# Batch 1's attention scores in one piece, and its softmax one slot sooner, in a fused attention and feed-forward kernel

## The chip, the cores and the metric

One core of a Trainium2 chip runs the whole kernel. The metric is the device time of one execution in microseconds; the figure shown is the median of several runs.

## The reference

Everything is fp32. There are 8 batches of 8 heads, 576 tokens and 64 columns a head, and 32 memory slots for each head. The input arrays are `q`, `k`, `v`, `phi`, `w_in` and `w_out`.

```
a      = softmax(phi) over the 576 tokens
k_m    = a^T k,   v_m = a^T v                       (32 x 64 a head)
attn   = softmax(q k_m^T / 8) over the 32 slots
x      = attn v_m, heads side by side               (4608 x 512)
out    = silu(x w_in) w_out                         (w_in 512 x 2048, w_out 2048 x 512)
```

## The kernel before, in words

**Folding.** `attn v_m` is never formed. `v_m w_in` (256 memory rows by 2048 columns) is made for each batch by `p_mm`, so that the first layer is `ffn1`: the transposed attention (two groups of 128 rows by 576 tokens) against that product. To keep fp32's accuracy with fast matmuls, operands are split into a high and a low part, and three matmuls (high high, high low, low high) stand for one. The splits are work for ScalarE (high) and VectorE (low).

**Slots.** A batch is 16 slots, one for each 128 of the 2048 hidden columns `fc`. A slot has 12 matmuls `ffn1(fc)` (L634) into the PSUM tile `h`, the SiLU of `h` on ScalarE (L657 into `g`, L659 into `gleft`, for the 64 tokens beyond 512), the split of `g` on VectorE (cast L649, subtract L651, into `gparts`), and 12 matmuls of the second layer (L673), for the slot before, into four accumulators. `h` is one tile of two PSUM banks: the next `ffn1` must wait for `gleft` (L659) to have read it, and for whoever else reads the space beside it.

**What stands between.** At times given in slots and half slots, a table `events` puts in the attention of the next batch: phi's softmax, `e_mm` (k_m and v_m, L327 and L335), `e_tr` (their transpose `kvT`, written beside `h`, read from there by VectorE, L358, and by ScalarE, L359), the scores, the softmax over memory slots (`s_max` L416, `s_sub` L420, `s_exp` L424 on ScalarE, `s_sum` L428 to 430, `s_norm` L434), the transposes back (`s_back` L447) and the split of the result. `p_mm` makes the next columns of the folded product in the PSUM tile `bg`, which exists once and which `p_mm`, `e_mm` of batch 1 and the scores share. Batch 0 has its own times (`at_slot`, L718), since in it the weights are also still being loaded and converted: they come as 64-bit words, and `w_conv` (L166 to 177) turns each piece into fp32 by two ScalarE steps (L167, L169), two or three VectorE steps (L171, L173, L177), and for `w_out` the high half `wo_hi` (L175) on ScalarE. The weight pieces go through three buffers, and a new load is issued as one is free.

**Scores.** For batches 2 to 7, `s_all` makes them in one go in slot 10: 288 + 224 columns in `bg`, the last 64 beside `h`, then four transposes on VectorE. For batch 1, `s_mm` makes them in two halves of 288 columns, each through `bg`, in slots 9.5 and 11.5, each followed by two transposes (L402). A half of `q` is loaded by `load_q`; the second half of batch 1's comes in slot 7.5.

**Order.** TensorE's order is that of the program (`in_order(PE)`). So is SyncE's, which issues nearly all DMAs, and, from batch 1 on, ScalarE's. In batch 0 a scheduler orders what VectorE and ScalarE do. In batch 0 events of a whole slot come after two of the four tiles of the second layer (`finish`), those of a half slot after all four.

Of the kernel before, what the change touches and what calls it, by code (L numbers as in the profile page):

```python
# [10 lines left out]
F32 = mybir.dt.float32  # L11
# [8 lines left out]
P = 128  # L20
B, S, H, M, D = 8, 576, 8, 32, 64
HM = H * M
NR = H // 2
# [6 lines left out]
HALF = S // 2  # L30
# [18 lines left out]
def attn_ffn_kernel(  # L49
# [9 lines left out]
    nc = tc.nc  # L59
    const = ctx.enter_context(tc.tile_pool(name="const", bufs=1))  # L60
    sb = ctx.enter_context(tc.tile_pool(name="sb", bufs=2))
# [24 lines left out]
    def load(dst, src, few=False, queue=None):  # L86
        i = (queue or nc.sync).dma_start(dst, src)
        if few:
            tc.add_manual_dep(
                i.ins,  # L90
                loads[-DEEP].ins.name,
                mybir.DependencyInfo(mybir.DependencyClass.Sync, mybir.DependencyReason.DATA),
                reason="few at a time",
            )
        loads.append(i)
# [18 lines left out]
    def bgtile():  # L114
        return ps.tile([P, 2, 512], F32, tag="bg", name="bg", bufs=1)
# [88 lines left out]
    at = [dict() for _ in range(B)]  # L204
    live = {}

    def banks(b):
        if b == 0:
            return [ps.tile([P, 512], F32, tag="acc", name=f"first{i}", bufs=NI) for i in range(2)]
        bg = bgtile()  # L210
        return [bg[:, 0], bg[:, 1]]

    def beside_h(w):

        return [live["h"][:, i, HALF : HALF + w] for i in range(2)]
# [10 lines left out]
    def load_kv(b):  # L226
        queue = nc.scalar if b == 0 else None
        ts = []
        for c in range(FULLC):
            t = sb.tile([P, 2, NR, KVW], F32, tag="kv", name=f"kv{b}_{c}", bufs=FULLC)  # L230
            load(t.rearrange("p g r f -> p (g r f)"), kv[b, :, c * KVC : (c + 1) * KVC], queue=queue)
            ts.append(t)
        t = sb.tile([P, NR, KVW], F32, tag="kr", name=f"kr{b}", bufs=1)
        load(t.rearrange("p r f -> p (r f)"), kv[b, :, FULLC * KVC :], queue=queue)
        at[b]["kv"], at[b]["kr"] = ts, t

    def load_q(b, hf, few=False):
        t = sb.tile([P, NR, HALF], F32, tag="q", name=f"q{b}_{hf}", bufs=2)
        at[b]["q", hf] = t
        load(t.rearrange("p r s -> p (r s)"), qT[b, hf], few)  # L240
# [121 lines left out]
    def s_all(b):  # L362

        sc = at[b]["sc"] = sb.tile([P, 2, S], F32, tag="att", name=f"sc{b}")
        bg, left = bgtile(), beside_h(S - 512)
        kvT = at[b]["kvT"]
        w = 512 - HALF
        for hf, f, n in ((0, 0, HALF), (1, 0, w), (1, w, HALF - w)):
            for r in range(NR):
                for p in range(2):  # L370
                    to = left[p] if f else bg[:, p, hf * HALF : hf * HALF + n]
                    nc.tensor.matmul(  # L372
                        to[M * r : M * (r + 1)],
                        kvT[D * p : D * (p + 1), 0, r],
                        at[b]["q", hf][D * p : D * (p + 1), r, f : f + n],
                        start=True, stop=True, skip_group_check=True,
                    )
        for p in range(2):
            nc.vector.transpose(sc[:, p, :512], bg[:, p])
        for p in range(2):  # L380
            nc.vector.transpose(sc[:, p, 512:], left[p])

    def s_mm(b, hf):
        if "sc" not in at[b]:
            at[b]["sc"] = sb.tile([P, 2, S], F32, tag="att", name=f"sc{b}")
        pt = banks(b)
        kvT, q = at[b]["kvT"], at[b]["q", hf]
        for r in range(NR):
            for p in range(2):
                nc.tensor.matmul(  # L390
                    pt[p][M * r : M * (r + 1), :HALF],
                    kvT[D * p : D * (p + 1), 0, r],
                    q[D * p : D * (p + 1), r],
                    start=True, stop=True, skip_group_check=True,
                )
        at[b]["sp", hf] = pt
        if b:
            s_turn(b, hf)

    def s_turn(b, hf):  # L400
        for p in range(2):
            nc.vector.transpose(at[b]["sc"][:, p, hf * HALF : (hf + 1) * HALF], at[b]["sp", hf][p][:, :HALF])  # L402

    def s_view(b, u):
        return at[b]["sc"][:, :, u[0] : u[1]].rearrange("p g (n m) -> p g n m", m=M)
# [183 lines left out]
    def p_mm(b, f, w, low=True):  # L589
        j = f // JW  # L590
        if f % JW == 0:
            pj[b, j] = [pparts[:, k, j % 2].rearrange("p (g f) -> p g f", g=2) for k in range(2)]
        hi, lo = pj[b, j]
        c = slice(f % JW, f % JW + w)
        bg = bgtile()
        kvT = at[b]["kvT"]
        for r in range(NR):
            for p in range(2):
                nc.tensor.matmul(  # L599
                    bg[M * r : M * (r + 1), p, :w].rearrange("p (k f) -> p k f", f=P),  # L600
                    kvT[D * p : D * (p + 1), 1, r],
                    win[D * p : D * (p + 1), f // P : (f + w) // P, r],
                    start=True, stop=True, skip_group_check=True,
                )
        if low:
            p_split(b, f, w, bg)
        return bg
# [97 lines left out]
    def ev(b, slot, fn, *a):  # L705
        events.setdefault((b, slot), []).append((fn, a))

    for b in range(B):
        n = b + 1
        if b == 0:  # L710
            for j in range(2, DFF // CW):
                ev(b, 2 * j - 1.5, p_mm, b, j * CW, CW)
        else:
            for j in range(1, NJ):
                ev(b, 4 * j - 3, p_mm, b, j * JW, JW)
        if n == B:
            continue
        at_slot = (4, 5, 6, 7.5, 9, 9.5, 11.5, 11.5, 12, 12.5, 12.5, 13) if b == 0 else (1, 2, 3, 5, 9, 10, 10, 11, 12, 13, 13, 14)  # L718
        mx, sub, ex, em, tr, s0, s1, sx, se, ss, sn, sk = at_slot
        ev(b, mx, phi_max, n)  # L720
        if n == 1:
            ev(b, sub, phi_allmax, n, (0, 1), (0,))
            ev(b, sub + 0.5, phi_allmax, n, (0, 1), (1,))
        else:
            for i in range(3):
                ev(b, sub, phi_fold, n, i)
        ev(b, sub + 0.5, phi_sub, n)
        ev(b, ex, phi_exp, n)
        ev(b, em, e_mm, n)
        if n + 1 < B:  # L730
            ev(b, 14 if b == 0 else em + 1, load_kv, n + 1)
        ev(b, tr, e_tr, n)
        ev(b, em, load_q, n, 1)
        if n == 1:
            ev(b, s0, s_mm, n, 0)
            ev(b, s1, s_mm, n, 1)
        else:
            ev(b, s0, s_all, n)
        if n + 1 < B:
            ev(b, s1, load_q, n + 1, 0)  # L740
        ev(b, sx, s_max, n, ALL)
        ev(b, sx, s_sub, n, ALL)
        ev(b, se, s_exp, n, ALL)
        ev(b, ss, s_sum, n, ALL)
        ev(b, sn, s_norm, n, ALL)
        ev(b, sk, s_back, n, ALL)
        ev(b, sk, s_low, n, ALL)
        if n + 1 < B:
            ev(b, sk, load_phi, n + 1)
        ev(b, 14, p_mm, n, 0, JW)  # L750
# [13 lines left out]
    with in_order(DVE, ACT) as last:  # L764
# [56 lines left out]
        bg = p_mm(0, 0, CW, False)  # L821
# [34 lines left out]
    load_next()  # L856
    load_kv(1)
    load_q(1, 0)
    for e in (DVE, ACT):
        whole.enter_context(tc.issue_after(last[e]))  # L860

# [36 lines left out]
def build(arrays, bacc, num_devices=1):  # L898
    nc = bacc.Bacc("TRN2", target_bir_lowering=False, num_devices=1, dynamic_dma_scratch_size=1024)
    aps = [  # L900
        nc.dram_tensor(n, a.shape, mybir.dt.from_np(a.dtype), kind="ExternalInput").ap() for n, a in arrays.items()
    ]
    out = nc.dram_tensor("out", (B * S, DMODEL), F32, kind="ExternalOutput").ap()
    with tile.TileContext(nc) as tc:
        attn_ffn_kernel(tc, *aps, out)
    return nc
# [44 lines left out]
```

## Time and profile before

| | before |
|---|---|
| median of 3 runs | 704.92 us (704.52 to 708.04) |
| the profiled execution | 704.6 us |
| its span, first to last instruction | 702.8 us |
| TensorE (PE) busy | 690.1 us, 98% |
| VectorE (DVE) busy | 366.1 us, 52% |
| ScalarE (ACT) busy | 258.7 us, 37% |
| HBM traffic | 49.95 MB read, 9.44 MB written |

A busy share is that of the whole span. Batch 0 takes the first 110 us or so, and VectorE and ScalarE are far busier in it than later: VectorE 4.96 of the 5 us from 95 to 100, for instance. A PE that is busy is issuing matmuls, which are pipelined; a row of the timeline merges neighbours (x12), its second number is the time until the last of them ends, and the time from one row's start to the next is what a stage costs. PEld is the weight load of a matmul.

### The profile page before, as it was taken

How to read it: one execution, taken by the hardware profiler on the slowest of the kernel's cores; microseconds unless marked ns; L12 is line 12 of the kernel's file. 1: busy time of each engine (PE TensorE's matmuls, PEld its weight loads, DVE VectorE, ACT ScalarE, POOL GpSimd, SP SyncE). 2: the span in 40 equal slices, each digit the busy share in tenths (PEclk: the TensorE clock that was granted, in tenths of full speed). 3: DMA queues.
4: the chain of work that ended last, by engine and by line, in shares of the span. 5: the costliest groups of instructions: out<-in, count | busy, mean ns of one | idle time of the engine just before them, and what ended most of it. 6: DMA issues, size and time to landing. Idle time of an engine off the chain costs nothing.

```text
span 702.8 us, 11778 instructions
## 1 busy us (share of the span) xinstructions
PE 690.1 (98%) x4924; PEld 562.7 (80%) x4924; DVE 366.1 (52%) x667; ACT 258.7 (37%) x455; POOL 0.7 (0%) x6
## 2 busy tenths in 40 slices
PE   8899989999999999999999999999999999999997
PEld 3578768888888888888888888888888888888885
DVE  4898796525745256634636346552564525623322
ACT  3779574413414124431413224341341412431211
POOL 0000000000000000000000000000000000000000
PEclk9999999999999999999999999999999999999999
DMA  9895726122210321131110311112121000010002
GB/s 334 306 341 188 254 78 230 36 102 68 71 39 12 126 68 35 61 137 54 48 61 16 136 39 55 71 40 97 68 76 34 1 1 1 1 61 1 1 0 76
DMA packets 25445, 60.15 MB, mean 86 GB/s; under 512 B 2096, under 2 KB 10416, under 8 KB 25392
## 3 DMA queue, kind: packets, MB, share of 16 engines
q1 hardware_dynamic: 24448, 56.63, 22.7%
q10 hardware_dynamic: 944, 2.77, 1.1%
q8 instruction: 39, 0.64, 0.4%
q14 instruction: 14, 0.11, 0.0%
HBM read 49.95 MB, written 9.44 MB: 85 GB/s over the span
## 4 chain that ended last, share of the span: by engine, by line
PE 85%; DVE 1%; ACT 0%; issue 0%; ACTq 0%
PE acc L673 46%; PE h L634 26%; PE accleft L673 6%; PE bg L599 4%; PE h L327 2%; PE bg L372 1%; PE h L335 0%; PE h L357 0%; ACT L657 0%; DVE sc L420 0%; DVE wo_lo L177 0%; DVE raw L173 0%; PE h L372 0%; ACT wo_hi L175 0%; DVE sc L402 0%
## 5 line engine op out<-in xcount | busy, mean ns | idle before, releaser
L673 PE MATMUL acc<-wo_hi,gparts 128*128 128x512 f32 x1024 | 342.1, 395 | 0.9 <-DVE gparts L651 0.5
L673 PEld LDWEIGHTS acc<-wo_hi,gparts 128*128 128x128 f32 x1024 | 192.2, 188 | 53.9 <-issue 6.6
L634 PEld LDWEIGHTS h<-aparts,pparts 128*128 128x128 f32 x1524 | 214.0, 188 | 15.0 <-issue 2.5
L634 PE MATMUL h<-aparts,pparts 128*128 128x288 f32 x1524 | 223.1, 295 | 1.5 <-ACT gleft L659 1.2
L657 ACT ACTIVATE g<-h 128x512 f32<-128x512 f32 x127 | 76.0, 598 | 348.7 <-PE h L634 179.8
L673 PE MATMUL acc<-wo_lo,gparts 128*128 128x512 f32 x512 | 201.0, 393 | 0.6 <-DVE wo_lo L177 0.6
L649 DVE CAST gparts<-g 128x512 fp32r<-128x512 f32 x128 | 54.5, 426 | 261.3 <-ACT g L657 261.2
L673 PEld LDWEIGHTS acc<-wo_lo,gparts 128*128 128x128 f32 x512 | 96.1, 188 | 18.3 <-DVE wo_lo L177 1.9
L651 DVE TENSOR_TENSOR gparts<-g,gparts 128x512 fp32r<-128x512 f32 x128 | 88.2, 689 | 10.6 <-DVE gparts L649 0.5
L615 DVE TENSOR_TENSOR pparts<-bg,pparts 128x1024 fp32r<-128x1024 f32 (+1 forms) x36 | 39.7, 1102 | 5.2 <-ACT pparts L613 4.8
L673 PE MATMUL accleft<-wo_hi,gparts 128*128 128x512 f32 x128 | 40.6, 390 | 0.0
L613 ACT ACTIVATE pparts<-bg 128x1024 fp32r<-128x1024 f32 (+1 forms) x36 | 33.6, 932 | 14.2 <-PE bg L599 14.1
L599 PE MATMUL bg<-win,kvT 64*32 64x512 f32 (+1 forms) x576 | 35.8, 554 | 0.0
L673 PEld LDWEIGHTS accleft<-wo_hi,gparts 128*128 128x128 f32 x128 | 24.0, 188 | 4.9
L659 ACT ACTIVATE gleft<-h 128x64 f32<-128x64 f32 x127 | 27.8, 219 | 0.0
L681 ACT ACTIVATE o<-acc 128x512 f32<-128x512 f32 x32 | 19.2, 599 | 21.9 <-PE acc L673 10.6
L673 PE MATMUL accleft<-wo_lo,gparts 128*128 128x512 f32 x64 | 24.9, 390 | 0.0
L657 ACT ACT_TABLE_LOAD x14 | 18.0, 1283 | 14.3 <-issue 13.8
L649 DVE CAST gparts<-gleft 128x512 fp32r<-128x512 f32 x16 | 6.8, 427 | 20.7 <-PE accleft L673 12.2
L169 ACT ACTIVATE raw<-raw 128x1024 int32<-128x1024 uint32 (+1 forms) x16 | 16.7, 1041 | 0.0
L327 PEld LDWEIGHTS h<-kv,phi 128*32 128x32 f32 x384 | 10.2, 110 | 5.0 <-ACT gleft L659 5.0
L673 PEld LDWEIGHTS accleft<-wo_lo,gparts 128*128 128x128 f32 x64 | 12.0, 188 | 2.4
(143 smaller groups left out, 366.1 us busy)
## 6 DMA issues: line engine op xcount, KB each, us to landing
kv<-in_kv SPq DMA_DIRECT2D x28, 516.0 KB, 5.6
q<-in_q SPq DMA_DIRECT2D x16, 576.0 KB, 4.9
out<-o SPq DMA_DIRECT2D x32, 256.0 KB, 2.1
raw<-in_w_in SPq DMA_DIRECT2D x14, 512.0 KB, 6.3
raw<-in_w_out SPq DMA_DIRECT2D x6, 1024.0 KB, 5.5
phi<-in_phi SPq DMA_DIRECT2D x7, 576.0 KB, 3.5
kv<-in_kv ACTq DMA_DIRECT2D x4, 516.0 KB, 6.7
kr<-in_kv SPq DMA_DIRECT2D x7, 258.0 KB, 6.6
```

The costliest lines, as they stand in the source:

```text
L169: i = nc.scalar.activation(r, low, AF.Copy, scale=2.0**-29)
L327: nc.tensor.matmul(pt[p][M * r : M * (r + 1), :KVW], e[:, p, c, M * r : M * (r + 1)], kvt[c][:, p, r], start=c == 0, stop=False, skip_grou ...
L599: nc.tensor.matmul(bg[M * r : M * (r + 1), p, :w].rearrange("p (k f) -> p k f", f=P), kvT[D * p : D * (p + 1), 1, r], win[D * p : D * (p + ...
L613: nc.scalar.activation(hi[:, :, c], bg[:, :, :w], AF.Copy)
L615: nc.vector.tensor_tensor(lo[:, :, c], bg[:, :, :w], hi[:, :, c], op=ALU.subtract)
L634: nc.tensor.matmul(h[:, hf, :HALF], wt[:, p, fs], a[:, p, hf * HALF : (hf + 1) * HALF], start=n[hf] == 0, stop=n[hf] == 5, skip_group_chec ...
L649: nc.vector.tensor_copy(ghi, g32)
L651: nc.vector.tensor_tensor(glo, g32, ghi, op=ALU.subtract)
L657: nc.scalar.activation(g32.rearrange("p (h f) -> p h f", h=2), h[:, :, :w], AF.Silu)
L659: i = nc.scalar.activation(gleft[:, fc, o : o + LEFT].rearrange("p (h f) -> p h f", h=2), h[:, :, w:HALF], AF.Silu)
L673: nc.tensor.matmul(acc[key], gt[:, cs], wt[:, fc], start=fc == 0 and n == 0, stop=fc == NFC - 1 and n == 2)
L681: nc.scalar.activation(o[:, :w], a[:, :w], AF.Copy)
```

## The change

Batch 1's scores are made by `s_all` too, in slot 10, so `s_mm` and `s_turn` go. `s_all` traces the transposes of the 64 columns beside `h` ahead of those of `bg` for batch 1. The softmax's steps of batch 1 move in the table for batch 0: `s_max` and `s_sub` from 11.5 to 10.5, the exp from 12 to 11, sum and normalise from 12.5 to 12; the way back stays at 13. The second half of batch 1's `q` is loaded right behind the first, ahead of the loop.

```diff
--- before.py
+++ after.py
@@ -375,31 +375,10 @@
                         at[b]["q", hf][D * p : D * (p + 1), r, f : f + n],
                         start=True, stop=True, skip_group_check=True,
                     )
-        for p in range(2):
-            nc.vector.transpose(sc[:, p, :512], bg[:, p])
-        for p in range(2):
-            nc.vector.transpose(sc[:, p, 512:], left[p])
-
-    def s_mm(b, hf):
-        if "sc" not in at[b]:
-            at[b]["sc"] = sb.tile([P, 2, S], F32, tag="att", name=f"sc{b}")
-        pt = banks(b)
-        kvT, q = at[b]["kvT"], at[b]["q", hf]
-        for r in range(NR):
+        parts = [(slice(512, S), left), (slice(0, 512), [bg[:, p] for p in range(2)])]
+        for cols, src in parts if b == 1 else parts[::-1]:
             for p in range(2):
-                nc.tensor.matmul(
-                    pt[p][M * r : M * (r + 1), :HALF],
-                    kvT[D * p : D * (p + 1), 0, r],
-                    q[D * p : D * (p + 1), r],
-                    start=True, stop=True, skip_group_check=True,
-                )
-        at[b]["sp", hf] = pt
-        if b:
-            s_turn(b, hf)
-
-    def s_turn(b, hf):
-        for p in range(2):
-            nc.vector.transpose(at[b]["sc"][:, p, hf * HALF : (hf + 1) * HALF], at[b]["sp", hf][p][:, :HALF])
+                nc.vector.transpose(sc[:, p, cols], src[p])
 
     def s_view(b, u):
         return at[b]["sc"][:, :, u[0] : u[1]].rearrange("p g (n m) -> p g n m", m=M)
@@ -715,7 +694,7 @@
                 ev(b, 4 * j - 3, p_mm, b, j * JW, JW)
         if n == B:
             continue
-        at_slot = (4, 5, 6, 7.5, 9, 9.5, 11.5, 11.5, 12, 12.5, 12.5, 13) if b == 0 else (1, 2, 3, 5, 9, 10, 10, 11, 12, 13, 13, 14)
+        at_slot = (4, 5, 6, 7.5, 9, 10, 10, 10.5, 11, 12, 12, 13) if b == 0 else (1, 2, 3, 5, 9, 10, 10, 11, 12, 13, 13, 14)
         mx, sub, ex, em, tr, s0, s1, sx, se, ss, sn, sk = at_slot
         ev(b, mx, phi_max, n)
         if n == 1:
@@ -730,12 +709,9 @@
         if n + 1 < B:
             ev(b, 14 if b == 0 else em + 1, load_kv, n + 1)
         ev(b, tr, e_tr, n)
-        ev(b, em, load_q, n, 1)
-        if n == 1:
-            ev(b, s0, s_mm, n, 0)
-            ev(b, s1, s_mm, n, 1)
-        else:
-            ev(b, s0, s_all, n)
+        if b:
+            ev(b, em, load_q, n, 1)
+        ev(b, s0, s_all, n)
         if n + 1 < B:
             ev(b, s1, load_q, n + 1, 0)
         ev(b, sx, s_max, n, ALL)
@@ -856,6 +832,7 @@
     load_next()
     load_kv(1)
     load_q(1, 0)
+    load_q(1, 1)
     for e in (DVE, ACT):
         whole.enter_context(tc.issue_after(last[e]))
 
```

The table `at_slot` and the scheduler set what these lines do to the queues; so here is the order on the two engines concerned, before and after (line numbers are each file's own; in the changed file the lines from `s_view` on are 21 less).

ScalarE, from the SiLU of slot 11 to `gleft` of slot 12. `g` and `gleft` are the SiLU's two results; `win`, `raw`, `cva` and `wo_hi` belong to the weights' conversion; `sc` is the exp of the softmax; numbers behind a name count buffers. Before:

```order
L657 ACTIVATE g_933<-h 128x512
L659 ACTIVATE gleft<-h 128x64
L167 ACTIVATE win<-raw 128x1024
L169 ACTIVATE raw<-raw 128x1024
L167 ACTIVATE cva<-raw 128x1024
L169 ACTIVATE raw<-raw 128x1024
L175 ACTIVATE wo_hi<-cva 128x1024
L657 ACTIVATE g_990<-h 128x512
L659 ACTIVATE gleft<-h 128x64
```

ScalarE, the same place after the change:

```order
L636 ACTIVATE g_956<-h 128x512
L638 ACTIVATE gleft<-h 128x64
L403 ACT_TABLE_LOAD
L403 ACTIVATE sc_891<-sc_891 128x1152
L167 ACTIVATE win<-raw 128x1024
L169 ACTIVATE raw<-raw 128x1024
L167 ACTIVATE cva<-raw 128x1024
L169 ACTIVATE raw<-raw 128x1024
L636 ACT_TABLE_LOAD
L636 ACTIVATE g_998<-h 128x512
L175 ACTIVATE wo_hi<-cva 128x1024
L638 ACTIVATE gleft<-h 128x64
```

The exp and the two table loads around it stand between the SiLU of slot 11 and that of slot 12; before, they stood two further instructions and an eviction of `p_mm` behind `gleft` of slot 12. `wo_hi` has moved between `g` and `gleft` of slot 12.

VectorE, around slot 10, from a step of the weights' conversion to the split of the `p_mm` of slot 10.5 (`pparts`). Before:

```order
L171 TENSOR_SCALAR cva<-cva 128x1024
L402 STREAM_TRANSPOSE sc_860<-bg 128x288 x2
L173 ISA raw<-raw,cva 128x1024x2
L649 CAST gparts<-g_892 128x512
L177 TENSOR_TENSOR wo_lo<-raw,wo_hi 128x1024
L651 TENSOR_TENSOR gparts<-g_892,gparts 128x512
L615 TENSOR_TENSOR pparts<-bg,pparts 128x2x256
```

VectorE, the same place after the change (`smx` is the maximum over the memory slots):

```order
L171 TENSOR_SCALAR cva<-cva 128x1024
L173 ISA raw<-raw,cva 128x1024x2
L177 TENSOR_TENSOR wo_lo<-raw,wo_hi 128x1024
L628 CAST gparts<-g_880 128x512
L630 TENSOR_TENSOR gparts<-g_880,gparts 128x512
L381 STREAM_TRANSPOSE sc_891<-bg 128x512
L381 STREAM_TRANSPOSE sc_891<-h 128x64 x2
L381 STREAM_TRANSPOSE sc_891<-bg 128x512
L395 TENSOR_REDUCE smx<-sc_891 128x36
L399 TENSOR_TENSOR sc_891<-sc_891,smx 128x1152
L594 TENSOR_TENSOR pparts<-bg,pparts 128x2x256
```

The transposes have moved behind the split of `g` of slot 10, and all four come at once, with the maximum and the subtraction right behind them.

On TensorE, 8 matmuls of 288 columns go from slot 9.5 and 8 from slot 11.5; 24 come in slot 10, between the second layer's first two tiles and its last two: 8 each of 288, 224 and 64 columns (the profile's rows count each of them twice). The `p_mm` of slot 10.5 follows six matmuls later. On SyncE the load of the second half of `q` moves from behind a late weight piece to right behind that of the first.

## Rows read from the trace of the kernel before

**Rows 1.** The page, part 1: busy us (share of the span) and instructions of each engine.
```profile
PE 690.1 (98%) x4924; PEld 562.7 (80%) x4924; DVE 366.1 (52%) x667; ACT 258.7 (37%) x455; POOL 0.7 (0%) x6
```

**Rows 2.** Chain that ended last, in time, one slot of batch 1: start us, us, what.
```profile
142.10 1.58 PE h L634 x12
...
146.43 1.58 PE h L634 x12
```

**Rows 3.** Timeline of TensorE, batch 0, slot 13: start us, us, engine, what, [idle before <-releaser].
```profile
94.06 1.85 PE L634 MATMUL h<-aparts,pparts 128*128 128x288 f32 x12
96.29 0.50 PE L673 MATMUL acc<-wo_hi,gparts 128*128 128x512 f32 x1 [0.37 <-DVE gparts L649]
...
101.21 1.85 PE L634 MATMUL h<-aparts,pparts 128*128 128x288 f32 x12 [1.16 <-ACT gleft L659]
```

**Rows 4.** Timeline of TensorE, batch 0, slots 9.5 to 11.
```profile
77.98 0.72 PE L390 MATMUL bg<-q,kvT 64*32 64x288 f32 x16
78.62 1.86 PE L634 MATMUL h<-aparts,pparts 128*128 128x288 f32 x12
...
83.18 0.66 PE L599 MATMUL bg<-win,kvT 64*32 64x256 f32 x16
83.77 1.85 PE L634 MATMUL h<-aparts,pparts 128*128 128x288 f32 x12
```

**Rows 5.** Timeline of TensorE, batch 1, slot 10 (scores of batch 2).
```profile
162.31 1.09 PE L372 MATMUL bg<-q,kvT 64*32 64x288 f32 x32
...
163.52 0.50 PE L673 MATMUL acc<-wo_hi,gparts 128*128 128x512 f32 x1
```

**Rows 6.** Timeline of ScalarE, batch 0, slots 5 and 9.
```profile
55.31 1.13 ACT L167 ACTIVATE cva<-raw 128x1024 f32<-128x1024 f32 x1
...
77.82 0.27 ACT L359 COPY kvT<-h 128x128 f32<-128x128 f32 x1
...
79.05 1.17 ACT L169 ACTIVATE raw<-raw 128x1024 int32<-128x1024 uint32 x1
```

**Rows 7.** Timeline of VectorE, batch 0, slots 10 to 12.
```profile
80.58 1.19 DVE L173 CUSTOM_DVE_ANT_0 raw<-raw,cva 128x2048 uint16<-128x2048 uint16 x1
...
83.16 0.68 DVE L651 TENSOR_TENSOR gparts<-g,gparts 128x512 fp32r<-128x512 f32 x1
...
94.54 1.35 DVE L420 TENSOR_TENSOR sc<-sc,smx 128x1152 f32<-128x1152 f32 x1
```

**Rows 8.** Timeline of VectorE, batch 1, slot 10.
```profile
164.24 1.31 DVE L379 STREAM_TRANSPOSE sc<-bg 128x512 f32<-128x512 f32 x2
...
165.47 0.34 DVE L381 STREAM_TRANSPOSE sc<-h 128x64 f32<-128x64 f32 x2
```

**Rows 9.** Timeline of ScalarE, batch 0, slots 11 to 13.
```profile
85.72 0.60 ACT L657 ACTIVATE g<-h 128x512 f32<-128x512 f32 x1 [1.18 <-PE h L634]
...
86.32 1.14 ACT L167 ACTIVATE win<-raw 128x1024 f32<-128x1024 f32 x1
...
90.50 1.05 ACT L175 ACTIVATE wo_hi<-cva 128x1024 fp32r<-128x1024 f32 x1
91.45 0.59 ACT L657 ACTIVATE g<-h 128x512 f32<-128x512 f32 x1
...
94.24 0.60 ACT L613 ACTIVATE pparts<-bg 128x512 fp32r<-128x512 f32 x1
94.86 1.28 ACT L424 ACT_TABLE_LOAD   x1
96.15 1.17 ACT L424 ACTIVATE sc<-sc 128x1152 f32<-128x1152 f32 x1
```

**Rows 10.** Windows: us, busy us of PE, PEld, DVE, ACT, POOL; granted clock, DMA share, GB/s.
```profile
40.00:45.00 5.00, 4.61 (x39) 3.52 (x39) 4.97 (x8) 3.50 (x6) 0.00 (x0) 1.00 1.03 381
...
100.00:105.00 5.00, 3.84 (x35) 2.82 (x34) 5.00 (x9) 1.86 (x5) 0.00 (x0) 1.00 0.00 0
```

**Rows 11.** Timeline of SyncE's queue (issues of DMAs), batch 0, slot 4.
```profile
46.86 0.38 SPq L87 DMA_DIRECT2D raw<-in_w_out  x1
```

## The prediction

> **What bounds the kernel now.** I read the page's busy shares first, then the TensorE timeline of the first batch, then what ScalarE and VectorE did under each hole in it. TensorE is busy 690.1 of 702.8 us [rows 1], so the kernel can gain only where TensorE stands idle, 12.7 us in all. An undisturbed slot (12 matmuls of `ffn1`, 1.58 us, and 12 of the second layer, 2.75) lasts 4.33 us from one `ffn1` to the next [rows 2]. The end of batch 0, where batch 1's softmax falls, does not run like that: `ffn1(13)` starts at 94.06 and `ffn1(14)` at 101.21, 7.15 us later [rows 3]. The row at 96.29 waited for VectorE's cast of `g(12)`, the one at 101.21 for ScalarE's `gleft(13)`, held up behind the softmax and its two table loads. After a stretch of narrow tiles the next `ffn1` takes some 0.1 us more, so this stretch loses 7.15 - 4.33 - 0.1 = **2.7 us**. That is all the change can win back there; the rest hangs on whether TensorE meets new waits.
>
> **The change, term by term.** TensorE runs in its written order, so I walk along it from slot 9 on, which the change leaves alone (`kvn` comes later on ScalarE, but its reader, the transpose in slot 9, comes some 4 us after).
>
> *Removed.* The holes at the end of batch 0: with the softmax done one slot sooner, VectorE and ScalarE reach slots 13 and 14 with the casts and `gleft` in time. **-2.7 us**, if nothing is late there.
>
> *Matmuls.* Two `s_mm` go, each 77.98 to 78.62, 0.64 us [rows 4]. One `s_all` comes; batch 2's takes 162.31 to 163.52, 1.21 us [rows 5]. Each turn to narrow tiles and back costs about 0.2 us (78.62 to 83.18 is 4.56, against 4.33 [rows 2, 4]), and there is one turn fewer. 1.21 - 1.28 - 0.2: **-0.3 us**.
>
> *A lost cover in slot 9.* Before, `s_mm` stood between the transpose into `h` and `ffn1(10)`, which overwrites `h`. TensorE came free for it at about 77.9 [rows 4]. ScalarE's copy of the second half of `kvT` out of `h` runs 77.82 to 78.09 [rows 6] and was hidden by those 0.64 us. Now `ffn1(10)` is next and waits for it, until 78.14 with the handover: 0.25 us, and some 0.1 us more because a matmul after a hole starts slowly. **+0.35 us** (0.2 to 0.5).
>
> *A new wait on bg in slot 10.5.* `bg` is one buffer. `p_mm(10.5)` needs it six matmuls after `s_all` has filled it; before, a whole slot lay between `s_mm` and the next user. TensorE: `ffn1(10)` at 78.14, 1.7 us, two tiles 1.37, `s_all` with its turn 1.3, two tiles 1.5: it wants `p_mm` at 84.0. VectorE: the conversion of `w_out` (`raw`, L173) starts when ScalarE ends its half at 79.05 + 1.17 = 80.22 [rows 6]; up to and with the second split of `g(10)` the four instructions took 80.58 to 83.84 [rows 7], 3.3 us, so now they end at 83.55. Then come the transposes, which in batch 2 take 1.31 us for two of 512 columns and 0.34 for two of 64, less an overlap 1.57 together [rows 8]. `bg` is free at 85.15. **+1.1 us** (0.3 to 1.5, a few tenths in each of the two chains). Queued behind the waiting `p_mm` is `ffn1(11)`, and behind it all of slot 11, so nothing takes up this wait.
>
> *A new wait on gleft(12) in slot 12.5.* `ffn1(11)` now starts at 85.85. `g(11)` follows 1.95 us behind, as at 83.77 and 85.72, and with `gleft` takes 0.60 to the next start [rows 4, 9]: 88.4. Then, in ScalarE's new order: a table load and the exp, 1.29 + 1.08 [rows 9]; four conversions, 86.32 to 90.50, 4.18; the table load back, 1.29; `g(12)`, `wo_hi` (90.50 to 91.45, 0.95) and only then `gleft(12)`, together 1.65. That ends at 97.9. VectorE isn't last there: max and subtract of 1.35 each [rows 7] are through by 87.9, before the first table load is. TensorE: `ffn1(11)` 85.85, one slot with the slow start 4.43, `ffn1(12)` at 90.3, another 4.33, the turn and `p_mm` 0.7, so `ffn1(13)` wants to start at 95.3. It needs `h` free of `gleft(12)` and starts at 97.95. **+2.65 us**, and 0.1 for the slow start. Bounds: 2.0 to 3.2, some 6% of the ten instructions either way. Before, `g(12)` came at 91.45, ahead of the exp at 96.15.
>
> *Late next.* VectorE's order puts the normalise and `wo_lo` ahead of the second split of `g(12)`; it ends near 99.7, and TensorE reads it near 100.2. Half a microsecond to spare: zero. `ffn1(14)` comes 4.5 us after `ffn1(13)`, at 102.45, against 101.21. For batch 1's first `ffn1`, two slots on, VectorE has only two transposes, one split and the casts left. So the 1.2 us stay.
>
> *Queues.* SP issues one more `q` load (576 KB) ahead of the weights, in a stretch in which the DMA engines are full at 381 GB/s [rows 10]: 1.5 us of transfer. The next weights (1 MB, 2.8 us at that rate) are issued at 46.86 [rows 11] and first read at 55.31 [rows 6], 8.4 us later; there is room. Zero, and 1.5 us if that cover is gone. The `q` load that leaves slot 7.5 frees SP for an issue; nothing waited for it. Batch 2's `q` and `phi` loads come with their slots, with a batch to spare: zero.
>
> *The sum.* -2.7 - 0.3 + 0.35 + 1.1 + 2.75 = **+1.2 us**. The profiled execution took 704.6 us; its span of 702.8 grows to 704.0, the 1.8 us around it stay: 705.8. The median of the runs shown, 704.92, is 0.3 above that execution, so I say **706.0 us**. About 0.5% (3.5 us) is what a measurement of this kernel can tell from no change; by that bound this is no change.
>
> [...] The chain of the last wait holds two table loads. In this trace the load at 94.86 starts 0.02 us after the eviction before it ends (94.24 + 0.60) and the exp starts at 96.15, 0.01 after the load [rows 9]: a switch costs 1.29 us and no more, which is what the sum takes. [...]
>
> **The rivals.**
> *1. The new waits don't form, the gain stays.* For it: 85.15 against 84.0 and 97.9 against 95.3 are chains of many durations, and a few tenths on each side move them. If the two small waits go, 706.0 - 1.45 = 704.6; if `gleft(12)` were in time too, 701.8. Against it: ScalarE's order stands, and ten instructions of known length between `g(11)` and `gleft(12)` can't be done in the 6.9 us that TensorE gives them. That the change doesn't do what it says belongs here: VectorE's order keeps one 512-column transpose ahead of those of the 64 columns, so `h` isn't freed first; but TensorE waits for `bg` then, and `h` costs nothing.
>
> *2. Weights come late.* If the `q` load pushes the weights read at 55.31 by its whole 1.5 us and the room isn't there, TensorE's waits for `wo_lo` in the slots behind grow by it: 707.5.
>
> [...]
>
> *4. Slower: TensorE's clock falls in the hole.* [...] No row here shows a drop.
>
> **How the numbers follow.** Forecast 74%; rival 1 13%, most of it at 704.6; rival 2 6%; rivals 3 and 4 3% each; 1% for what I don't see. Faster by over 0.5% means below 701.4, which only the whole of rival 1 with a good run would reach: 0.02. Slower by over 0.5% means above 708.4: rivals 3 and 4 and the far end of rival 2, 0.08. The rest, 0.90, is no change. The bounds of the terms reach from 1.6 below the forecast (0.15 on the copy, 0.8 on `bg`, 0.65 on `gleft`) to 1.1 above it. With the spread of the runs shown (0.4 below the median) and rival 2, the range is 703.8 to 708.0.
>
> **What would show it.** Right: TensorE idle some 1.1 us ahead of `p_mm` in slot 10.5, released by VectorE's transpose, and some 2.65 us ahead of `ffn1(13)`, released by `gleft`; none between `ffn1(13)` and `ffn1(15)`. Wrong: `ffn1(13)` before 96, so that ScalarE's chain is shorter than worked out; idle ahead of a table load; a clock below 1.00; waits for `wo_lo` grown in the slots before 9.

## The result and the profile after

| | before | after |
|---|---|---|
| median | 705.02 us, 20 runs | 707.88 us, 20 runs |
| lowest to highest | 704.20 to 708.04 | 705.99 to 710.45 |
| ratio to before | | 1.0036 (95%: 1.0028 to 1.0044) |
| the profiled execution, its span | 704.6, 702.8 us | 706.24, 704.5 us |

The kernel is slower by 0.36%, inside the 0.5% that the prediction counted as no change. The range of 703.8 to 708.0 holds the median, barely; the forecast of 706.0 is 1.9 us below it.

The profile first. TensorE in the changed kernel, slots 10 to 15 (the six L613 rows are `ffn1(10)` to `ffn1(15)`), against [rows 3, 4] (start, us, what, [idle before <-releaser]):

```profile
78.25 1.86 PE L613 MATMUL h<-aparts,pparts 128*128 128x288 f32 x12
...
85.64 0.67 PE L578 MATMUL bg<-win,kvT 64*32 64x256 f32 x16 [1.42 <-DVE sc L381]
86.24 1.85 PE L613 MATMUL h<-aparts,pparts 128*128 128x288 f32 x12
...
90.66 1.75 PE L613 MATMUL h<-aparts,pparts 128*128 128x288 f32 x12
...
98.55 1.86 PE L613 MATMUL h<-aparts,pparts 128*128 128x288 f32 x12 [2.81 <-ACT gleft L638]
100.26 0.39 PE L652 MATMUL acc<-wo_hi,gparts 128*128 128x512 f32 x1
...
103.00 1.75 PE L613 MATMUL h<-aparts,pparts 128*128 128x288 f32 x12
...
108.57 1.75 PE L613 MATMUL h<-aparts,pparts 128*128 128x288 f32 x12
```

Both new waits are there, at the places forecast, and between `ffn1(13)` and `ffn1(15)` there is none: the holes of [rows 3] are gone. `ffn1(15)` starts at 108.57, against 106.89 in the trace before: 1.7 us later, and the span is 1.7 longer.

The chain under the 2.81 us, on ScalarE, against [rows 9], and ahead of it the copy out of `h` in slot 9:

```profile
77.90 0.29 ACT L359 COPY kvT<-h 128x128 f32<-128x128 f32 x1
...
88.69 0.22 ACT L638 ACTIVATE gleft<-h 128x64 f32<-128x64 f32 x1
88.92 1.28 ACT L403 ACT_TABLE_LOAD   x1
90.22 1.17 ACT L403 ACTIVATE sc<-sc 128x1152 f32<-128x1152 f32 x1
91.29 1.12 ACT L167 ACTIVATE win<-raw 128x1024 f32<-128x1024 f32 x1
92.29 1.15 ACT L169 ACTIVATE raw<-raw 128x1024 int32<-128x1024 uint32 x1
93.33 1.15 ACT L167 ACTIVATE cva<-raw 128x1024 f32<-128x1024 f32 x1
94.36 1.17 ACT L169 ACTIVATE raw<-raw 128x1024 int32<-128x1024 uint32 x1
95.55 1.28 ACT L636 ACT_TABLE_LOAD   x1
96.84 0.60 ACT L636 ACTIVATE g<-h 128x512 f32<-128x512 f32 x1
97.34 1.05 ACT L175 ACTIVATE wo_hi<-cva 128x1024 fp32r<-128x1024 f32 x1
98.28 0.22 ACT L638 ACTIVATE gleft<-h 128x64 f32<-128x64 f32 x1
```

No row of the chain waits for anything: nine instructions stand back to back between the first `gleft` and the second. `ffn1(12)`, which the first one let go, started at 90.66; TensorE was ready for `ffn1(13)` at 95.7, and the second `gleft` ends at 98.50. Each table load starts 0.01 to 0.02 us after the instruction ahead of it ends, and what it is for 0.01 to 0.02 after it.

The chain under the wait on `bg`, on VectorE, against [rows 7, 8]:

```profile
80.32 1.23 DVE L173 CUSTOM_DVE_ANT_0 raw<-raw,cva 128x2048 uint16<-128x2048 uint16 x1 [0.36 <-ACT raw L169]
81.66 1.23 DVE L177 TENSOR_TENSOR wo_lo<-raw,wo_hi 128x1024 fp32r<-128x1024 f32 x1
82.80 0.42 DVE L628 CAST gparts<-g 128x512 fp32r<-128x512 f32 x1
83.32 0.69 DVE L630 TENSOR_TENSOR gparts<-g,gparts 128x512 fp32r<-128x512 f32 x1
83.93 0.71 DVE L381 STREAM_TRANSPOSE sc<-bg 128x512 f32<-128x512 f32 x1
...
84.83 0.67 DVE L381 STREAM_TRANSPOSE sc<-bg 128x512 f32<-128x512 f32 x1
```

So far this is the forecast with 0.5 us more (704.5 for the span, where 704.0 was forecast). But the profiled execution was one of the quickest, and the runs say something else. Of the 20 executions 5 have a mean granted clock of 1.000 and took 705.99 to 706.70; the other 15 have 0.994 to 0.998 and took 707.50 to 710.45. The median belongs to the second group, of which this trace shows nothing. Its executions lie 1.3 to 4.2 us above the 706.22 that is the middle of the first.

### The profile page after: what moved, and what is told of

The parts are those of the page before. It is cut to its first block, busy times and chain, and to the rows that moved or that the text cites. A ratio compares the mean times of both kernels' runs of the same rounds, so it can differ in the third digit from the quotient of the medians.

```text
span 704.5 us, 11807 instructions
## 1 busy us (share of the span) xinstructions
PE 689.0 (98%) x4940; PEld 563.0 (80%) x4940; DVE 366.7 (52%) x667; ACT 258.8 (37%) x455; POOL 0.7 (0%) x6
## 4 chain that ended last, share of the span: by engine, by line
PE 89%; ACT 2%; DVE 1%; issue 1%; ACTq 0%; DVEq 0%
PE acc L652 48%; PE h L613 27%; PE accleft L652 6%; PE bg L578 4%; PE h L327 2%; PE bg L372 1%; DVE wo_lo L177 1%; ACT raw L169 0%; PE h L335 0%; PE h L357 0%; ACT cva L167 0%; ACT win L167 0%; ACT wo_hi L175 0%; PE bg L327 0%; DVE sc L381 0%
## 5 line engine op out<-in xcount | busy, mean ns | idle before, releaser
L613 PEld LDWEIGHTS h<-aparts,pparts 128*128 128x128 f32 x1524 | 214.1, 188 | 16.1 <-ACT gleft L638 3.3
L613 PE MATMUL h<-aparts,pparts 128*128 128x288 f32 x1524 | 222.8, 295 | 3.3 <-ACT gleft L638 2.8
L630 DVE TENSOR_TENSOR gparts<-g,gparts 128x512 fp32r<-128x512 f32 x128 | 88.2, 689 | 10.5
L407 DVE TENSOR_REDUCE ssm<-sc 128x36 f32<-128x1152 f32 x7 | 9.5, 1354 | 9.6 <-ACT sc L403 9.6
```

What stands on the lines that cost most here:

```text
L613: nc.tensor.matmul(h[:, hf, :HALF], wt[:, p, fs], a[:, p, hf * HALF : (hf + 1) * HALF], start=n[hf] == 0, stop=n[hf] == 5, skip_group_chec ...
L630: nc.vector.tensor_tensor(glo, g32, ghi, op=ALU.subtract)
```

## The experiments

All were timed against the kernel before on the same chip; runs 1 to 4, 5 to 8 and 9 to 12 each had a chip of their own, on which the kernel before took 705.08, 704.89 and 705.00 us. The first four ask what sets those 15 executions apart.

**1. The changed kernel once more.** No edit.

> The changed kernel once more, beside the others of this chip. Two theories are told apart by these four runs. A, waits only: the three waits (kvT copy, bg, gleft of slot 12) are all that the change costs; the spread of the first runs, 15 of 20 with a mean granted clock of 0.994 to 0.998, belongs to the chip and not to the kernel. B, waits and clock: the 2.81 us hole ahead of ffn1(13) also lets the granted clock fall in most executions. A expects a median near 706.2 (the executions at clock 1.000 took 705.99 to 706.70) if this chip is quieter, or the same spread here and in the two kernels beside it without the hole. B expects about three quarters of the executions below 1.000 again, a median of 707.4 to 708.4, and in a profile that shows it a granted clock below 1.00 in or behind the stretch from 95 to 100.

Measured: 707.52 us (706.04 to 708.85), 5 runs, ratio 1.0037 (1.0024 to 1.0049). Four of five are above 707, so 19 of 25 in all. This time the profiled execution (707.19) is one of them. Its TensorE (start, us, what), and windows of the same stretch (us, busy us of PE, PEld, DVE, ACT, POOL; granted clock, DMA share, GB/s):

```profile
98.22 3.15 PE L613 MATMUL h<-aparts,pparts 128*128 128x288 f32 x12 [2.84 <-ACT gleft L638]
101.21 0.39 PE L652 MATMUL acc<-wo_hi,gparts 128*128 128x512 f32 x1
...
103.95 1.75 PE L613 MATMUL h<-aparts,pparts 128*128 128x288 f32 x12
```
```profile
96.00:97.00 1.00, 0.00 (x0) 0.00 (x0) 1.00 (x2) 0.99 (x2) 0.00 (x0) 1.00 0.00 0
97.00:98.00 1.00, 0.00 (x0) 0.00 (x0) 1.00 (x2) 1.00 (x3) 0.00 (x0) 0.84 0.00 0
98.00:99.00 1.00, 0.78 (x3) 0.78 (x4) 0.98 (x2) 1.00 (x4) 0.00 (x0) 0.50 0.00 0
...
100.00:101.00 1.00, 1.00 (x6) 1.00 (x5) 1.00 (x2) 0.79 (x1) 0.00 (x0) 0.50 0.00 0
101.00:102.00 1.00, 1.00 (x6) 0.87 (x6) 0.12 (x1) 0.60 (x2) 0.00 (x0) 0.95 0.00 0
```

The granted clock goes from 1.00 to 0.50 while TensorE stands in the hole, and is back at about 101.1. In between lies `ffn1(13)`: from its start to the next row it takes 2.99 us, against 1.71 (98.55 to 100.26) in the profile at full clock. The fall costs **1.3 us** here, behind the wait. This was the quickest of the four; no trace was kept of the others, two of which have a mean clock of 0.994 and took over 708.5.

**2. The hole filled.** What is added in `p_mm`:

```diff
+        if b == 0 and f == 14 * P:
+            for _ in range(20):
+                nc.tensor.matmul(bg[:, 0, 2 * P :], dummy[:, :P], dummy, start=True, stop=True)
```

> The changed kernel with 20 matmuls of 256 columns, whose results nothing reads, behind p_mm of slot 12.5 in the unused half of bg: by the 512-column ones at the kernel's start they should take some 2.2 of the 2.81 us in which TensorE waits for gleft(12). ffn1(13) starts no sooner, so the span at full clock stays 704.5 (704.2 to 704.9). A (waits only) expects no other time: the same spread and the same median as the changed kernel beside it. B (waits and clock) expects every execution at clock 1.000 and a median of 706.2 (705.9 to 706.7), 1.0 to 2.0 below the changed kernel beside it.

Measured: 706.22 us (705.57 to 706.69), 11 runs, ratio 1.0014 (1.0006 to 1.0023). TensorE's rows:

```profile
95.51 2.36 PE L586 MATMUL bg<-ident 128*128 128x256 bf16 x20
98.41 1.86 PE L616 MATMUL h<-aparts,pparts 128*128 128x288 f32 x12 [0.54 <-ACT gleft L641]
```

`ffn1(13)` starts where it did, and none of 11 executions is above 707: the spread is gone, and 1.3 us of the median with it. B holds and A falls. On this chip the change costs 2.44 us, then: 1.14 by its waits and 1.30 by the clock. The means of B's forecast were too strict: some are 0.998 or 0.999, as in the kernel before. Such a mean can come from the end of the program, where TensorE has no work left: in the eighth run's profile (mean 0.998) its last matmul ends at 697.1, and the clock is 1.00 up to 695, 0.91 from there to 700 and 0.50 from 700 to the end at 701.6.

**3. A hole by itself.** The kernel before, with this in `silu`, ahead of `gleft`:

```diff
+        if b == 3 and fc == 7:
+            for n in (1024,) * 4 + (512,):
+                t = sb.tile([P, 2 * DMODEL], F32, tag="cva", name="t", bufs=1)
+                nc.scalar.activation(t[:, :n], win[:, :2].rearrange("p k r f -> p (k r f)")[:, :n], AF.Copy)
```

> The kernel before with one hole made by itself, far from batch 0: in batch 3, slot 7, five extra ScalarE copies (four of 1024 columns at 1.05 us each, one of 512 at 0.5, results unused) stand between the SiLU of g and of gleft. gleft ends 4.7 us later; 1.77 us of that are slack there (gleft ends 2.56 after ffn1 starts, the next ffn1 comes 4.33 after it), so TensorE waits 2.9 us ahead of ffn1(8), released by gleft. A expects the kernel before plus 2.9 to 3.1 us, 708.0, in nearly every execution, with a clock of 1.000. B expects in most executions a mean clock of 0.994 to 0.998 and 1 to 3 us on top: a median of 709 to 711.

Measured: 709.87 us (707.91 to 710.19), 5 runs, ratio 1.0064 (1.0051 to 1.0076): four at 709.56 or more with means of 0.997 and 0.998, one at 707.91 with 0.999. The profiled one, TensorE and windows:

```profile
321.13 2.54 PE L634 MATMUL h<-aparts,pparts 128*128 128x288 f32 x12 [2.99 <-ACT gleft L663]
...
327.15 1.75 PE L634 MATMUL h<-aparts,pparts 128*128 128x288 f32 x12
```
```profile
320.00:322.00 2.00, 0.87 (x6) 0.87 (x7) 0.00 (x0) 1.05 (x3) 0.00 (x0) 1.00 0.00 0
322.00:324.00 2.00, 2.00 (x10) 1.90 (x9) 0.00 (x0) 0.29 (x1) 0.00 (x0) 0.50 0.00 0
324.00:325.00 1.00, 1.00 (x4) 0.81 (x3) 0.55 (x2) 0.42 (x2) 0.00 (x0) 0.50 0.00 0
```

The slot behind the hole takes 6.02 us, with softmax, weights and batch 0 far away; behind a shorter hole at the same place, without a fall, it takes 4.43 (run 7 below). The fall costs **1.6 us** here. So the hole does it, not what surrounds it in slot 12. Here the clock fell at 322.0, just after TensorE had come back to work; all of the half rate fell on matmuls, and the price is higher than in run 1.

**4. The chain shortened.** Of the list of conversion slots one entry moves:

```diff
+    OVER = {('i', 7): 10.5}
-    ... [2 * j - 1 if k == "i" else ...
+    ... [OVER.get((k, i), 2 * j - 1 if k == "i" else ...
```

> The changed kernel with the conversion of the last piece of w_in one half slot sooner, in slot 10.5 instead of 11: on ScalarE its two steps (2.05 us) leave the chain between g(11) and gleft(12) and fall into the 4.58 us in which ScalarE stood idle before pparts of slot 10.5; on VectorE its shift (0.6) now stands between cast and split of g(10), ahead of the transposes. Both theories expect the wait on bg at 1.4 to 2.0 and the one on gleft(12) at 0.3 to 1.0, so a span at full clock of 702.6 to 703.6. A expects a median 1.2 below the changed kernel beside it, with the same spread of clocks. B expects all executions at clock 1.000 and a median of 704.4 to 705.4, 2.5 to 3.3 below the changed kernel beside it.

Measured: 705.19 us (704.38 to 706.35), 11 runs, ratio 1.0001 (0.9992 to 1.0010), 2.33 below run 1: a little under B's span of gains and twice A's. TensorE's two waits:

```profile
86.64 0.67 PE L578 MATMUL bg<-win,kvT 64*32 64x256 f32 x16 [1.84 <-DVE sc L381]
...
97.50 1.85 PE L613 MATMUL h<-aparts,pparts 128*128 128x288 f32 x12 [0.74 <-ACT gleft L638]
```

The change without its long hole is as fast as the kernel before. B's clock of 1.000 in all executions was again too strict: four have 0.996 or 0.998, of which three took no longer than the rest.

**5. One part alone: scores in one go, softmax at its old slots.**

```diff
-        at_slot = (4, 5, 6, 7.5, 9, 10, 10, 10.5, 11, 12, 12, 13) if b == 0 ...
+        at_slot = (4, 5, 6, 7.5, 9, 10, 10, 11.5, 12, 12.5, 12.5, 13) if b == 0 ...
```

> The changed kernel with the softmax of batch 1 at the slots it had before (s_max and s_sub at 11.5, the exp at 12, sum and normalise at 12.5), so that of the change only the scores in one go and the early load of q are left. Does the loss come from the scores or from the softmax being one slot sooner? If the softmax sooner is to blame (it puts exp and table loads ahead of gleft(12)), the wait ahead of ffn1(13) goes; the one on bg stays at 1.1 to 1.5. But walking along the order, the exp and its two table loads then stand ahead of gleft(13), and the hole comes back one slot later, 2.0 to 3.0 us ahead of ffn1(14), with 0.4 to 0.8 more for the split of g(13): a span at full clock of 704.5 to 705.5 and, if theory B (holes let the clock fall) holds, a median of 706.5 to 708.5. If the scores in one go cost nothing by themselves, the span is that of the kernel before or less, 702.5.

Measured: 707.50 us (706.51 to 708.08), 6 runs, ratio 1.0033 (1.0021 to 1.0044). TensorE:

```profile
86.49 0.67 PE L578 MATMUL bg<-win,kvT 64*32 64x256 f32 x16 [1.43 <-DVE sc L381]
...
103.50 1.86 PE L613 MATMUL h<-aparts,pparts 128*128 128x288 f32 x12 [2.36 <-ACT gleft L638]
106.25 0.74 PE L652 MATMUL acc<-wo_hi,gparts 128*128 128x512 f32 x2 [0.41 <-DVE gparts L630]
```

As expected: no wait ahead of `ffn1(13)`, the same on `bg`, and the hole one slot later. Where the softmax stands decides mainly which `gleft` is late. Three of the six executions have a mean clock of 0.996 or 0.997. The profiled one (707.57) isn't among them: behind the hole of 2.36 us `ffn1(14)` takes 1.70 us to the next row (103.50 to 105.20), against 1.71 for `ffn1(13)` in the profile after, which is at full clock. It is late by its waits, and by some 0.9 us that arose before (the transposes into `h` of slot 9 start at 77.22, in the profile after at 76.36); its span of 705.8 is above the 704.5 to 705.5 expected.

**6. One part alone: the early load of `q`.** The kernel before with `load_q(1, 1)` behind `load_q(1, 0)`.

> The kernel before with one part of the change alone: the second half of batch 1's q loaded right behind the first. My prediction put this at zero; its rival at 1.5 us, by which weights arrive late. Expected: a median within 0.4 of the kernel before (705.1); by the rival 706.6, with longer waits for wo_lo in the slots before 9.

Measured: 704.76 us (704.52 to 705.36), 11 runs, ratio 0.9997 (0.9989 to 1.0006). TensorE's wait for `wo_lo` at 63.1 is 0.18 us with and without it. No cost of the load shows.

**7. A shorter hole.** Run 3 with `(1024,) * 3`.

> The kernel before with the hole of the third run made shorter: three extra ScalarE copies of 1024 columns between g and gleft in batch 3, slot 7, instead of five. TensorE should wait 3 x 1.05 - 1.77, so 1.3 to 1.5 us, ahead of ffn1(8). If the granted clock falls in a hole of this length too, the median is the kernel before plus 2.5 to 3.5 us, 708, with a stretch of rows at 0.50; if it falls only in the longer one, plus 1.3 to 1.6, 706.5, with no such stretch behind the hole.

Measured: 706.53 us (706.14 to 708.18), 11 runs, ratio 1.0023 (1.0014 to 1.0032); the hole is 1.24 us:

```profile
319.26 1.85 PE L634 MATMUL h<-aparts,pparts 128*128 128x288 f32 x12 [1.24 <-ACT gleft L663]
...
323.69 1.74 PE L634 MATMUL h<-aparts,pparts 128*128 128x288 f32 x12
```

Ten executions are at 706.65 or less, which is the wait, the slow start (4.43 us from this `ffn1` to the next, against 4.33 [rows 2]) and a few tenths; one is at 708.18 with a mean of 0.997.

**8. The wait on `bg` attacked too.** Run 4, and `split` of slot 10 traced behind the scores, with an order (no semaphore) that puts it and the shift of the moved piece behind the last transpose:

```diff
-            gs = split(silu(b, fc, h))
+            g32 = silu(b, fc, h)
+            late = (b, fc) == (0, 10)
+            gs = None if late else split(g32)
...
+                if late and part == 0:
+                    gs = split(g32, first_slot=True)
...
+            if first_slot:
+                behind(i, ("turn", 1))
```

> The kernel of the fourth run (last piece of w_in converted in slot 10.5) with the wait on bg attacked as well: the cast and split of g(10) and the shift of that piece stand behind the four transposes on VectorE instead of ahead of them (1.7 us of work). Theory: the wait on bg is made by what VectorE does ahead of the transposes, and nothing takes its place; then it falls from 1.84 to 0.1 to 0.5, ffn1(13) still waits 0.3 to 1.0, and the median is 1.2 to 2.0 below the fourth run's, 703.2 to 704.0, the first version below the kernel before. Rival: VectorE is full in this stretch and what it does later is late in turn; then the wait moves to the second layer of slot 11 (split of g(10)) or to ffn1(12) (pparts), and the median stays at 704.8 to 705.6.

Measured: 703.36 us (702.75 to 706.05), 11 runs, ratio 0.9984 (0.9973 to 0.9995). TensorE and, ahead of it, VectorE:

```profile
84.89 0.67 PE L590 MATMUL bg<-win,kvT 64*32 64x256 f32 x16 [0.30 <-DVE sc L393]
...
95.72 1.87 PE L625 MATMUL h<-aparts,pparts 128*128 128x288 f32 x12 [0.71 <-ACT gleft L652]
```
```profile
82.03 1.23 DVE L179 TENSOR_TENSOR wo_lo<-raw,wo_hi 128x1024 fp32r<-128x1024 f32 x1
83.18 0.71 DVE L393 STREAM_TRANSPOSE sc<-bg 128x512 f32<-128x512 f32 x1
```

The wait on `bg` goes from 1.84 to 0.30, nothing takes its place, and the median is 1.8 below run 4's (1.6 when each is taken against the kernel before on its chip). The rival, VectorE being full, falls: it is busy in this stretch, but what was put off had time. Three of the 11 executions are above 705: one with a mean clock of 0.993, two with 1.000, which stay unexplained.

**9. The same order alone, without the earlier conversion.**

> The changed kernel with one half of the eighth run alone: cast and split of g(10) behind the four transposes, the conversion of the last piece of w_in where the change has it (slot 11). Do the two waits add up, one behind the other, or does the later one hide the earlier? By the prediction's step nothing takes up the wait on bg: then it falls from 1.42 to 0.1 to 0.5, all of slot 11 comes 1.1 sooner, ScalarE's chain starts that much sooner too, and the wait on gleft(12) stays 2.6 to 2.9: 0.5 to 1.2 us less than the changed kernel at equal clock (an execution at full clock 705.0 to 705.7), the clock falling in most executions as there, a median of 706.2 to 707.3. Rival: ScalarE's chain to gleft(12) doesn't start sooner, the hole grows by what bg gives back, and the median is that of the changed kernel, 707.5 to 708.0.

Measured: 706.10 us (705.60 to 707.74), 12 runs, ratio 1.0017 (1.0008 to 1.0025). The wait on `bg` is 0.31; the other, with the next `ffn1` behind it:

```profile
97.45 3.13 PE L623 MATMUL h<-aparts,pparts 128*128 128x288 f32 x12 [2.76 <-ACT gleft L650]
...
103.45 1.75 PE L623 MATMUL h<-aparts,pparts 128*128 128x288 f32 x12
```

From `ffn1(10)` to `ffn1(13)` it is 19.15 us, against 20.30 in the profile after. So, by the rows, the two waits stand one behind the other and add up. The slot behind the hole takes 6.00 us, against 4.45 in the profile after: here too the fall costs some 1.6, and the granted clock went from 1.00 to 0.50 at 97.6, just after TensorE had come back to work. Seven of the 12 executions have a mean of 1.000 and took 705.60 to 706.12, only some 0.4 below the changed kernel's; where the rest of the 1.15 us goes can't be read from the profiled execution, whose clock fell.

**10. The conversion alone, in the kernel before.**

> The kernel before with the conversion of the last piece of w_in in slot 10.5 instead of 11, and nothing of the change. Is the gain of the eighth run the conversion's alone? If it is, this kernel too takes 703.2 to 704.0. If it needs the scores in one go and the softmax sooner, the holes of the end of batch 0 only move here: the cast and split of g(12) come in time, but gleft(13) is still late behind exp and table loads (0.8 to 1.2) and the split of g(13) behind it (up to 1.4), and the median is 704.4 to 705.2.

Measured: 704.51 us (703.63 to 705.36), 12 runs, ratio 0.9991 (0.9982 to 0.9999), 0.5 us below the kernel before. The waits are 1.00 on `gleft(13)` and 0.99 on the split of `g(13)`: the holes mostly just move, as expected.

**11. The kernel before with the conversion and the softmax sooner, scores in halves.** Run 4's entry in the list of conversion slots, and:

```diff
-        at_slot = (4, 5, 6, 7.5, 9, 9.5, 11.5, 11.5, 12, 12.5, 12.5, 13) if b == 0 ...
+        at_slot = (4, 5, 6, 7.5, 9, 9.5, 11, 11, 11.5, 12, 12, 13) if b == 0 ...
```

> The kernel before, with the same conversion in slot 10.5 and the softmax of batch 1 half a slot sooner (second half of the scores and s_max, s_sub at 11, the exp at 11.5, sum and normalise at 12), but the scores still in two halves. Is making the scores in one go needed for the gain of the eighth run? If only the softmax's time and the conversion matter, 0.7 to 1.3 us below the kernel before: 703.8 to 704.4. If the halves are in the way, 704.7 to 705.3.

Measured: 703.31 us (702.99 to 703.70), 9 runs, ratio 0.9972 (0.9963 to 0.9982), a little better than expected. One wait is left, 1.02 us on `gleft(13)`.

**12. Run 8 once more.**

> The eighth run's kernel once more, beside these three, since its first interval (0.9973 to 0.9995) nearly reached 1 and three of its 11 executions were above 705. Expected: a median of 702.8 to 703.8 and a ratio of 0.997 to 0.999. If the first result was luck of one chip: 704.5 or more.

Measured: 703.02 us (702.65 to 703.26), 6 runs, ratio 0.9968 (0.9956 to 0.9980). Runs 11 and 12 are both 0.3% faster than the kernel before, and so faster than the changed one. Their intervals overlap: the gain doesn't need the scores in one go.

## Why the prediction was right, and where it was not

- *Removed holes, -2.7:* right. `ffn1(13)` to `ffn1(14)` is 4.45 us, against 4.33 for an undisturbed slot [rows 2]; the 0.12 is the slow start (`ffn1(13)` takes 1.71 us to the next row, `ffn1(14)` behind it 1.58).
- *Matmuls, -0.3:* right. `s_all` takes 81.42 to 82.56, 1.14 us, where 1.21 was taken from batch 2.
- *Lost cover, +0.35:* right. `ffn1(10)` starts at 78.25, forecast 78.14, behind ScalarE's copy (77.90 to 78.19); some 0.1 us of lateness was there already at the transposes of slot 9.
- *Wait on `bg`, +1.1:* 1.42, inside its bounds. VectorE's transposes began at 83.93 instead of 83.55: the four instructions ahead of them started 0.1 later and took 3.6 us instead of the 3.3 of [rows 7].
- *Wait on `gleft(12)`, +2.65:* 2.81. The chain is the one listed; it ended 0.6 later than worked out, 0.4 of it because `ffn1(11)` had come that much later behind `bg`.
- *Nothing takes up the waits, nothing late next:* right by the rows, and the rows of run 9 show them adding up; its times give back only 0.4 of the 1.15 us.
- *Queues, zero:* right (run 6; the next weights were issued at 46.92, against 46.86 in [rows 11]). Rival 2 falls.
- *Table loads at 1.29:* right. From the start of a load to the start of what it is for it is 1.30 and 1.29 us in the rows of ScalarE above. Rival 3 has its 3% in the chances for ScalarE being idle ahead of both loads; no trace of this chain shows that: they start 0.01 and 0.02 us after the instruction ahead of them ends, and in run 4 both 0.02.

The waits come to +1.8 by the profiled executions (-2.7 - 0.3 + 0.45 + 1.42 + 2.9, the last with its slow start) and to +1.0 (0.4 to 1.6) by run 2, which has them without the fall; the forecast was +1.2.

**The step that failed is the chance of rival 4**, the falling clock: "No row here shows a drop", and 3%. The forecast took the granted clock of 1.00 over holes of up to 1.16 us [rows 3, 10] as evidence for one of 2.65, more than twice as long. That was an extrapolation. Run 7 (1.24 us, ten of 11 untouched) beside run 3 (2.99 us, one of five) shows that the two lengths behave differently, and run 1 showed one of the prediction's own signs of being wrong, a clock below 1.00. In the profiles of runs 1, 3 and 9 it falls to 0.50.

The chances put rival 4 above 708.4, more than 2.4 us over the forecast. No trace shows a term of that size: a whole slot at half rate would cost 4.3 us by [rows 2], as an estimate, and the three that show a fall give 1.3, 1.6 and 1.6 (runs 1, 3 and 9). Only the slowest of the 20 executions lost 4.2, and what the clock did in it isn't shown. With the traced prices the case would have been 706.0 + 1.3 to 1.6, so 707.3 to 707.6, and the likeliest.

So the forecast described the minority of executions, those at full clock, within 0.7 us, and the median of 707.88 lies in the range by luck: the bounds of the terms end at 707.1, and the rest up to 708.0 was put there for the spread of the runs and for rival 2, weights that come late, which run 6 excludes.

## What to carry to other kernels

Where a change joins several short waits into one long one on TensorE, count the long one dearer than its length: here 2.8 us cost at least 1.3 more, in three executions of four. One profile can miss this; look at the clocks and the spread of all runs. And before moving a step, look for what stands in the chain ahead of the late instruction and could run earlier, in time that its engine idles. Here neither part did much alone: the conversion moved by half a slot gained 0.5 us (run 10), and the rearranged scores and softmax lost 2.4 to 2.9 (run 1 and the result). Both together came out even (run 4); with VectorE's order mended they gained 2.0 (run 12), and with the scores in halves and the softmax only half a slot sooner 1.7 (run 11).

## What the runs showed that was not expected

Whether the clock falls differs from execution to execution of one kernel: rare behind the short holes, common behind the long ones, never in all. The longest hole in the stretch concerned, and the executions with a mean clock of 0.998 or less that also took at least 0.7 us more than the middle of those at 0.999 or 1.000 (a low mean alone doesn't count, since it can come from the end of the program):

| longest hole | kernel | with the fall |
|---|---|---|
| 1.16 us | before, beside runs 1 to 12 | 1 of 75 |
| 1.24 us | run 7 | 1 of 11 |
| 1.84 us | run 4 | 1 of 11 |
| 2.36 us | run 5 | 3 of 6 |
| 2.76 us | run 9 | 4 of 12 |
| 2.81, 2.84 us | after, run 1 | 19 of 25 |
| 2.99 us | run 3 | 4 of 5 |

Such a count rests on means: a trace shows the fall itself only in runs 1, 3 and 9, and where between the lengths it becomes common can't be read from so few.

The kernel filled with matmuls whose results nothing reads is faster than the same kernel without them, 706.22 against 707.52, though TensorE does 2.36 us more work and the wait's end doesn't move. And the same fall has two prices: 1.3 us where the clock fell while TensorE still stood (run 1), 1.6 where it fell just after work had begun (runs 3 and 9).
